# Top-k attention with an ELU feed-forward: scores three steps ahead in the opening, weight shifts a piece later in steps 8 to 10

## The chip, the cores and the metric

The kernel runs on one core of one Trainium2 chip. The metric is the device time of one execution in microseconds (us), the median of several runs. Before the change it is 1658.51 us, from three runs between 1657.33 and 1662.03.

A core has these engines: TensorE (PE) multiplies and transposes, VectorE (DVE) and ScalarE (ACT) work on rows of data, GpSimd (POOL) does small elementwise work here, and SyncE (SP) issues most transfers. Each engine works through its own list of instructions in order and waits at each for what it depends on.

## The reference

Attention over 8 batches, 8 heads, 576 positions and head size 64 keeps only the 32 largest scores of each row; its output, 4608 rows of 512, goes through a feed-forward layer with 2048 hidden columns and ELU.

```python
scores = scale * np.matmul(q, k.transpose(0, 1, 3, 2))
kth = np.partition(scores, -top_k, axis=-1)[..., -top_k:-top_k + 1]
scores = np.where(scores >= kth, scores, -1000000000.0)
attn = np.exp(scores - np.max(scores, axis=-1, keepdims=True))
attn = attn / (np.sum(attn, axis=-1, keepdims=True) + 1e-09)
x = np.matmul(attn, v)            # then (B,H,S,D) -> (B*S, H*D)
h = x @ w_in
g = np.where(h > 0.0, h, np.exp(np.minimum(h, 0.0)) - 1.0)
out = g @ w_out
```

The weights w_in and w_out come in as 64-bit floats.

## The kernel before

**Steps.** The work is a list of 144 steps (`steps`), each a tile of 128 query rows for a pair of heads. The main loop (line 667) walks over n and works at several steps at once: it computes scores for step n+2 (`scores(ahead)`), finds the 32 largest of step n (`select_row` or `select`), masks and exponentiates (`mask`), normalises step n-1 (`normalise`), transposes the weights (`turn`), and multiplies with v once a group of tiles is complete (`attend`).

**A step on each engine.** `scores(u)` is four matmul calls (L302) into two PSUM tiles, `wide[0]` and `wide[1]`, and two ACT copies (L310) into a buffer `sc`, of which there are five. The selection on DVE is four passes of the largest eight (L321, L331, or L344, L356) with three replacements between them (L325, L349), for two rows of heads. `mask` is ACT's L375, L378 and L379, or POOL's L377 in place of L375. `normalise` is POOL's L389 to L396. `turn` is nine transposes on PE (L415), in three groups (main, rest, other), each with an ACT copy (L416). The group `rest` shares the PSUM tile `wide[1]`. `attend` is L441 on PE and L468 on ACT.

**Feed-forward.** `ffn_pieces` makes a list of pieces for each block of rows: `hidden` (L513 on PE, then L523, L526, L528 on ACT) and `project` (L538 on PE, L547 on ACT, then the store). The sum that completes four hidden columns, L485 on DVE, is called a gate; it is emitted two quarter steps after its `hidden` piece. `feed` runs four times per step and takes pieces from the list by planned costs and due times. A piece is taken only if enough weights are decoded (`decoded[0]`): `project` of the first block and everything of later blocks wait for that.

**Weights.** The 64-bit weights are decoded in 32 pieces (2*NF), of which pieces 0 to 15 are w_in and 16 to 31 are w_out. Each passes through a load by SP (L153, into one of eight `raw` buffers), a clamp on POOL (`convert_first`, L174), three ACT instructions (`convert_second`, L180, L181, L183), a shift on DVE (`convert_third`, L187), and an addition on POOL (`convert_last`, L191). `hook` runs one entry of the list `decode`, `decode_piece(i)`: it issues the load of piece i+3 and the stages of pieces i, i-1, i-3 and i-4. Hooks stand between the selection passes: four per step for n = 0 to 6, none in n = 7, three per step from n = 8 until the list is empty. In this kernel entries 28 to 30 run in n = 8, 31 to 33 in n = 9, and the last, 34 and 35, in n = 10.

**Order.** For n below `tight` = 8 the framework's scheduler orders the instructions of each engine. From n = 8 on they stay in the order of the code, within a `manual_schedule`.

Of the kernel before, what the change touches and what calls it, by code (L numbers as in the profile page):

```python
# [81 lines left out]
def kernel(  # L82
# [17 lines left out]
    NHP = H // 2  # L100
    NC = dm // P
    NF = dff // P
# [48 lines left out]
    def load_weight(i):  # L151
        t = rawpool.tile([P, 2 * WN], U32, tag="raw", name="raw")
        nc.sync.dma_start(t[:], weight(i)[0])  # L153
        raw[i] = t
# [37 lines left out]

    decode = []
    decoded = [0]

    def hook():

        if not decode:
            return
        decode.pop(0)()  # L200
        if not decode:
            raws.close()
            late["f"] = ctx.enter_context(tc.tile_pool(name="f", bufs=2))
            late["g"] = ctx.enter_context(tc.tile_pool(name="g", bufs=2))
            late["x"] = ctx.enter_context(tc.tile_pool(name="xt", bufs=2))

    def decode_piece(i):
        if i + 3 < 2 * NF:
            load_weight(i + 3)
        for ago, stage in (  # L210
            (0, convert_first), (1, convert_second), (3, convert_third), (4, convert_last)
        ):
            if 0 <= i - ago < 2 * NF:
                stage(i - ago)
        decoded[0] = max(0, i - 3)

    loaded, kqT, vT = {}, {}, {}

# [18 lines left out]
    def load_v(b, hp):  # L237

        t = kvpool.tile([P, 2 * J + 2, D], FP32, tag="vT", name="vT")
        for hh in range(2):  # L240
            h = 2 * hp + hh
            nc.sync.dma_start(
                t[:, hh * J : (hh + 1) * J, :],
                v[b, h, 0:JP, :].rearrange("(p j) d -> p j d", j=J),
            )
            mine = slice(hh * R, (hh + 1) * R)
            other = slice((1 - hh) * R, (2 - hh) * R)
            nc.gpsimd.memset(t[other, 2 * J + hh, :], 0.0)
            nc.sync.dma_start(t[mine, 2 * J + hh, :], v[b, h, JP:S, :])
        vT[b, hp] = t  # L250
# [33 lines left out]
    def turn_qk(whole=False):  # L284
        while turning:
            if next(turning[0], turning) is turning:
                turning.pop(0)
            elif not whole:
                return
# [3 lines left out]
    def scores(u):  # L293

        u.sc = scpool.tile([P, 2, S], FP32, tag="sc", name="sc")
        q0 = QUERIES + u.t.qt * P
        for half in range(2):
            for h, i, rows in u.heads:
                kq = kqT[u.t.b, h // 2]
                part = slice(i * D, (i + 1) * D)  # L300
                k0 = (KEYS if i == 0 else 0) + half * HS
                nc.tensor.matmul(  # L302
                    wide[i][rows, half, 0:HS],
                    kq[part, q0 : q0 + u.t.ql],
                    kq[part, k0 : k0 + HS],
                    start=True,
                    stop=True,
                )
        for i in range(2):
            nc.scalar.activation(  # L310
                u.sc[:, i, :].rearrange("p (a s) -> p a s", a=2),
                wide[i][:, :, 0:HS], AF.Copy, scale=scale,
            )

    def select_row(u, i, decoding):
        if i == 0:
            u.first = small.tile([P, 2, 8], FP32, tag="m1", name="m1")
            u.last = small.tile([P, 2, 8], FP32, tag="m4", name="m4")
        sc = u.sc[:, i, :]
        m = u.first[:, i, :]  # L320
        nc.vector.max(m, sc)  # L321
        wk = wkpool.tile([P, S], FP32, tag=f"wk{i}", name="wk")
        cur = sc
        for r in range(TOP_K // 8 - 1):
            nc.vector.match_replace(wk[:], m, cur, TAKEN)  # L325
            cur = wk[:]
            if r < TOP_K // 8 - 2:
                m = small.tile([P, 8], FP32, tag=f"m{i}", name="m")[:]
            else:
                m = u.last[:, i, :]  # L330
            nc.vector.max(m, cur)  # L331
            if r > 0 and decoding:
                hook()
            if r != 1:
                yield
# [89 lines left out]
    def attend(g):  # L425
        t = g.tiles[0]
        ps = ps_t.tile([P, JP], FP32, tag="t", name="avps")
        n = P if t.rem else sum(x.ql for x in g.tiles)
        for k in range(2 if t.rem else 1):
            hp = 2 * g.hp + k if t.rem else g.hp  # L430
            vt = vT[t.b, hp]
            for c in range(J + 1):
                for i in range(2):
                    chunk = J if c == J else i * (J + 1) + c
                    w = g.et[:, chunk, :, :].rearrange("p a q -> p (a q)")
                    cols = slice(0, n)
                    if t.rem:
                        c0 = R * (k if i == 0 else 1 - k)
                        w = w[:, c0 : c0 + R]
                        cols = slice(k * R, (k + 1) * R)  # L440
                    nc.tensor.matmul(  # L441
                        ps[i * D : (i + 1) * D, cols],
                        vt[:, 2 * J + i if c == J else i * J + c, :],
                        w,
                        start=(c == 0),
                        stop=(c == J),
                    )
        if t.rem:
            finish(t.block, 2, slice(2 * g.hp, 2 * g.hp + 2), t.cols,
                   ps[:, 0:n].rearrange("p (a q) -> p a q", a=2))  # L450
            return
        c0 = 0
        tiles = list(g.tiles)
        while tiles:
            blk, lo, parts = tiles[0].block, tiles[0].cols.start, 0
            while tiles and tiles[0].block is blk:
                parts += 1
                hi = tiles.pop(0).cols.stop
            finish(blk, parts, g.hp, slice(lo, hi), ps[:, c0 : c0 + hi - lo])
            c0 += hi - lo  # L460
# [105 lines left out]
    blocks, tight = [], 2 * NHP  # L566
    for b in range(B):
# [28 lines left out]
        for qts in order:  # L596
# [3 lines left out]
            for qt in qts:  # L600
                n = len(steps)
# [9 lines left out]
    def at(step, fn, *args):  # L611
        todo.setdefault(step, []).append((fn, args))
# [42 lines left out]
    load_qk(0, 3)  # L655
    for hp in range(1, NHP):
        load_v(0, hp)
    decode += [lambda i=i: decode_piece(i) for i in range(2 * NF + 4)]
    at(0, start_qk, 0, 2)
    at(1, start_qk, 0, 3)  # L660

    def step(n):
        return steps[n] if 0 <= n < NS else None
# [3 lines left out]
    for n in range(NS + 3):  # L667
        for fn, args in todo.pop(n, []):
            fn(*args)
        ahead, cur, prev, done = step(n + 2), step(n), step(n - 1), step(n - 2)  # L670
        if n < tight:
            turn_qk(True)
            scores(ahead)
            for i in range(2):
                passes = select_row(cur, i, n < tight - 1)
                next(passes)
                if i == 0:
                    while closing:
                        attend(closing.pop(0))
                elif prev:  # L680
                    normalise(prev)
                    turn(prev, main)
                    turn(prev, rest)
                    turn(prev, other)
                feed(n, 0.25)
                next(passes)
                mask(cur, i, True)
                feed(n, 0.25)
            continue
        if n == tight:  # L690
            ctx.enter_context(tc.manual_schedule(engines=engines))
        passes = select(cur) if cur else iter(range(4))
        if ahead:
            scores(ahead)
        while closing:
            attend(closing.pop(0))
        next(passes)
        feed(n, 0.25)
        if prev:
            mask(prev, 0)  # L700
        turn_qk()
        next(passes)
        feed(n, 0.25)
        if done:
            turn(done, main)
            turn(done, rest)
        if prev:
            mask(prev, 1)
        next(passes)
        feed(n, 0.25)  # L710
        if done:
            turn(done, other)
        next(passes)
        if prev:
            normalise(prev)
        feed(n, 0.25)
        turn_qk(True)
# [36 lines left out]
```

## Time and profile before

| | |
|---|---|
| median of three runs | 1658.51 us |
| the profiled execution | 1660.99 us |
| its span, first to last instruction | 1659.2 us |
| PE busy | 1599.8 us (96%) |
| DVE busy | 1495.4 us (90%) |
| ACT busy | 1152.4 us (69%) |
| POOL busy | 574.9 us (35%) |
| granted PE clock, mean | 0.974 |

The profile is one execution. The span leaves out 1.8 us around the instructions. Busy shares are means over stages that differ: in the first 160 us the weights are decoded beside the attention steps; from about 1560 us on, only feed-forward work is left. The granted clock is the share of its full rate at which PE was allowed to run; a busy PE at half clock does half the work. In the rows of a timeline or a chain of waits the columns are start, length, engine, line and count. In a row of waits they are who waited for whom, the total, how often, and the longest.

### The profile page before, as it was taken

How to read it: one execution, taken by the hardware profiler on the slowest of the kernel's cores; microseconds unless marked ns; L12 is line 12 of the kernel's file. 1: busy time of each engine (PE TensorE's matmuls, PEld its weight loads, DVE VectorE, ACT ScalarE, POOL GpSimd, SP SyncE). 2: the span in 40 equal slices, each digit the busy share in tenths (PEclk: the TensorE clock that was granted, in tenths of full speed). 3: DMA queues.
4: the chain of work that ended last, by engine and by line, in shares of the span. 5: the costliest groups of instructions: out<-in, count | busy, mean ns of one | idle time of the engine just before them, and what ended most of it. 6: DMA issues, size and time to landing. Idle time of an engine off the chain costs nothing.

```text
span 1659.2 us, 25687 instructions
## 1 busy us (share of the span) xinstructions
PE 1599.8 (96%) x8528; PEld 1033.8 (62%) x8528; DVE 1495.4 (90%) x3044; ACT 1152.4 (69%) x2393; POOL 574.9 (35%) x1415
## 2 busy tenths in 40 slices
PE   5789999999999999999999999999999999999999
PEld 3566777666574757556566676756557575756564
DVE  6986999999999999999999999999999999998500
ACT  6887777678675867678667776768658585857521
POOL 4774334333333333333333233333323233332200
PEclk8588999999999999999999999999999999999999
DMA  7530110011100210011100110001200100000000
GB/s 229 184 115 7 42 39 22 7 25 40 42 1 7 50 50 8 7 28 37 36 14 1 49 36 29 0 22 36 50 13 1 34 9 29 7 7 7 7 13 13
DMA packets 101124, 56.19 MB, mean 34 GB/s; under 512 B 84096, under 2 KB 92288, under 8 KB 100992
## 3 DMA queue, kind: packets, MB, share of 16 engines
q1 hardware_dynamic: 99792, 54.26, 11.6%
q8 instruction: 68, 1.11, 0.3%
q14 instruction: 64, 0.52, 0.1%
q10 hardware_dynamic: 1200, 0.30, 0.1%
HBM read 45.09 MB, written 9.44 MB: 33 GB/s over the span
## 4 chain that ended last, share of the span: by engine, by line
PE 73%; DVE 18%; ACT 5%; POOL 2%; issue 1%; DMA 1%; SPq 0%; ACTq 0%; POOLq 0%; DVEq 0%
PE ops L538 26%; PE hps L513 23%; PE avps L441 8%; PE scps L302 7%; DVE wk L349 7%; DVE m L356 6%; PE eps L415 6%; DVE m L344 2%; PE qkps L272 1%; DVE gT L485 1%; ACT sc L379 1%; DVE wk L325 1%; PE scps L415 1%; ACT sc L378 1%; ACT et L416 1%
## 5 line engine op out<-in xcount | busy, mean ns | idle before, releaser
L356 DVE MAX8 m<-wk 128x8 f32<-128x576 f32 x816 | 574.8, 745 | 0.0
L513 PE MATMUL hps<-xT,w_in 128*128 128x256 f32 (+2 forms) x2432 | 546.9, 374 | 0.0
L538 PE MATMUL ops<-w_out,gT 128*128 128x512 f32 x1152 | 522.9, 598 | 0.0
L513 PEld LDWEIGHTS hps<-xT,w_in 128*128 128x128 f32 x2432 | 405.6, 192 | 98.2 <-issue 24.8
L349 DVE MATCH_REPLACE8 wk<-m,wk 128x576 f32<-128x576 f32 x544 | 399.3, 741 | 0.0
L538 PEld LDWEIGHTS ops<-w_out,gT 128*128 128x128 f32 x1152 | 209.0, 190 | 232.4 <-issue 219.7
L389 POOL TENSOR_SCALAR dene<-den 128x2 f32<-128x2 f32 x144 | 35.9, 249 | 815.7 <-ACT sc L379 815.2
L378 ACT ACTIVATE sc<-sc,m 128x576 f32<-128x576 f32 x288 | 226.9, 788 | 40.8 <-DVE m L356 40.5
L379 ACT ACTIVATE sc<-sc,den 128x576 f32<-128x576 f32 x288 | 223.5, 776 | 37.1 <-POOL den L377 12.5
L310 ACT ACTIVATE sc<-scps 128x576 f32<-128x576 f32 x288 | 173.3, 656 | 73.7 <-PE scps L302 73.5
L396 POOL TENSOR_SCALAR sc<-sc,rec 128x576 f32<-128x576 f32 x288 | 218.7, 770 | 14.9
L302 PE MATMUL scps<-kqT 64*128 64x288 f32 (+1 forms) x1280 | 205.9, 442 | 17.3 <-ACT kqT L278 8.7
L416 ACT COPY et<-eps 128x512 f32<-128x512 f32 x288 | 166.3, 577 | 78.5 <-PE eps L415 78.3
L441 PE MATMUL avps<-et,vT 128*64 128x256 f32 (+2 forms) x2080 | 196.8, 331 | 7.7 <-ACT et L416 7.6
L349 DVE MATCH_REPLACE8 wk<-m,sc 128x576 f32<-128x576 f32 x272 | 199.7, 741 | 0.0
L415 PEld LDWEIGHTS eps<-ident,sc 128*128 128x128 f32 x1152 | 143.6, 144 | 86.5 <-issue 47.4
L485 DVE SCALAR_TENSOR_TENSOR gT<-n,gT 128x512 f32<-128x512 f32 (+1 forms) x132 | 99.0, 750 | 108.2 <-ACT n L528 108.2
L415 PE MATMUL eps<-ident,sc 128*128 128x128 f32 x1152 | 176.8, 279 | 17.2 <-POOL sc L396 15.0
L344 DVE MAX8 m<-sc 128x8 f32<-128x576 f32 x272 | 191.0, 743 | 0.0
L441 PEld LDWEIGHTS avps<-et,vT 128*64 128x64 f32 x2080 | 124.3, 143 | 84.2 <-issue 26.1
L302 PEld LDWEIGHTS scps<-kqT 64*128 64x128 f32 (+1 forms) x1280 | 109.7, 182 | 89.4 <-issue 44.0
L523 ACT ACTIVATE n<-hps 128x512 f32<-128x512 f32 (+1 forms) x156 | 87.7, 562 | 84.2 <-PE hps L513 82.2
(49 smaller groups left out, 1086.4 us busy)
## 6 DMA issues: line engine op xcount, KB each, us to landing
kin<-in_k_dram SPq DMA_DIRECT2D x64, 128.0 KB, 2.8
raw<-in_moe_w_in_dram SPq DMA_DIRECT2D x16, 512.0 KB, 5.9
vT<-in_v_dram SPq DMA_DIRECT2D x64, 128.0 KB, 2.2
raw<-in_moe_w_out_dram SPq DMA_DIRECT2D x16, 512.0 KB, 3.5
out_dram<-osb SPq DMA_DIRECT2D x32, 256.0 KB, 2.3
qin<-in_q_dram SPq DMA_DIRECT2D x62, 128.0 KB, 2.8
kin<-in_k_dram SPq DMA_DIRECT2D x32, 32.0 KB, 2.5
vT<-in_v_dram SPq DMA_DIRECT2D x64, 16.0 KB, 2.1
```

Source lines behind the costliest of these rows:

```text
L302: nc.tensor.matmul(wide[i][rows, half, 0:HS], kq[part, q0 : q0 + u.t.ql], kq[part, k0 : k0 + HS], start=True, stop=True,)
L344: nc.vector.max(found[i], cur[i])
L349: nc.vector.match_replace(wk[i], found[i], cur[i], TAKEN)
L356: nc.vector.max(found[i], cur[i])
L378: nc.scalar.activation(sc, sc, AF.Prelu, scale=-1.0, bias=low, alpha=1.0 / STEEP)
L379: nc.scalar.activation(sc, sc, AF.Exp, scale=-STEEP, bias=gap, accum_out=u.den[:, i : i + 1])
L396: nc.gpsimd.tensor_scalar(u.sc[:, i, :], u.sc[:, i, :], rec[:, i : i + 1], 1.0, ALU.mult, ALU.mult)
L415: nc.tensor.transpose(ps[:, c * P : (c + 1) * P], sc[:, c0 : c0 + P], ident[:])
L416: nc.scalar.copy(g.et[:, chunks, u.at, :], ps[:, 0 : n * P].rearrange("p (c q) -> p c q", c=n),)
L441: nc.tensor.matmul(ps[i * D : (i + 1) * D, cols], vt[:, 2 * J + i if c == J else i * J + c, :], w, start=(c == 0), stop=(c == J),)
L513: nc.tensor.matmul(blk.h[:, f % bank, :], w_in[:, i, f * P : (f + 1) * P], blk.xT[:, i, 0:n_tok], start=(i == 0), stop=(i == NC - 1),)
L538: nc.tensor.matmul(blk.o[:], blk.gT[f // NG][:, f % NG, s * P : (s + 1) * P], w_out[:, f, :], start=(f == 0), stop=(f == NF - 1),)
```

## The change

Two things are changed.

First, the scores. In n = 0 and n = 1 scores of step n+2 are computed as before. In n = 2 they are computed for steps 4 and 5, and from n = 3 to n = 7 for step n+3. In n = 8 none are computed, since step 10 has been done; from n = 9 on it is step n+2 again.

Second, the weights. From entry `scheduled` = 28 on, that is from n = 8, the shift and the addition are done for pieces i-4 and i-5 instead of i-3 and i-4. Entry 28 does neither of the two, so no piece is skipped, and the list gets one entry more, 36, which runs in n = 10. `decoded[0]` follows.

```diff
     decoded = [0]
+    scheduled = 4 * (2 * NHP - 1)
...
-        for ago, stage in (
-            (0, convert_first), (1, convert_second), (3, convert_third), (4, convert_last)
-        ):
+        apart = 1 if i >= scheduled else 0
+        stages = [(0, convert_first), (1, convert_second)]
+        if i != scheduled:
+            stages += [(3 + apart, convert_third), (4 + apart, convert_last)]
+        for ago, stage in stages:
             if 0 <= i - ago < 2 * NF:
                 stage(i - ago)
-        decoded[0] = max(0, i - 3)
+        decoded[0] = max(0, i - 3 - apart)
...
-    decode += [lambda i=i: decode_piece(i) for i in range(2 * NF + 4)]
+    decode += [lambda i=i: decode_piece(i) for i in range(2 * NF + 5)]
...
         if n < tight:
             turn_qk(True)
-            scores(ahead)
+            if n < 3:
+                scores(ahead)
+            if n > 1:
+                scores(step(n + 3))
...
-        if ahead:
+        if ahead and n > tight:
             scores(ahead)
```

## The prediction

> Steps are numbered as in the code, n = 0 to 143; a piece is one of the 32 slices of weights; a gate is the VectorE (DVE) instruction of L485 that completes four hidden columns.
>
> **What bounds the kernel now.** I first read the busy time by stretch.
>
> ```profile
> 120.00:140.00 20.00, 16.57 (x67) 9.03 (x66) 11.06 (x23) 14.95 (x31) 11.13 (x20) 0.83 0.00 1
> 140.00:160.00 20.00, 17.41 (x95) 12.00 (x94) 15.96 (x33) 14.74 (x30) 10.58 (x21) 0.91 0.04 14
> 160.00:300.00 140.00, 139.18 (x1112) 101.47 (x1111) 138.65 (x286) 105.98 (x225) 48.53 (x132) 1.00 0.12 30
> 300.00:850.00 550.00, 538.72 (x2840) 344.65 (x2838) 550.00 (x1125) 393.17 (x818) 191.06 (x503) 0.99 0.10 26
> 850.00:1560.00 710.00, 706.51 (x3681) 448.59 (x3678) 673.95 (x1367) 499.61 (x1039) 231.53 (x609) 1.00 0.07 20
> ```
>
> Columns: length, then PE, weight loads, DVE, ACT, POOL busy, granted clock, DMA share, GB/s. From 300 to 850 us DVE never rests and PE has 11.3 us to spare; from 850 on PE is full and DVE waits. So a lead that DVE holds at 300 reaches the end if PE can make up its part from those 11.3 us. Before 160 nobody is full: there the change works. Next, what DVE waits for between 60 and 165 us:
>
> ```profile
> DVE gT L485 <- ACT n L528: 9.0, 3, 5.4
> DVE raw L187 <- POOL rec L394: 7.3, 1, 7.3
> DVE raw L187 <- ACT raw L181: 4.2, 3, 2.4
> ```
>
> The 7.3 us is one stall, 125.2 to 132.4, at the end of n = 8. The releaser named there is doubtful (POOL's L394 ended at 132.15): by the code the shift of piece 27 needs ACT's L181 of that piece, at 131.66. The 5.4 us is the first gate of the second block, at 161.35. The chain of waits tells who made both late:
>
> ```profile
> 123.89 0.67 PE eps L415 x4
> ...
> 126.14 2.29 PE scps L302 x6
> 128.42 2.33 PE avps L441 x20
> 130.75 7.69 PE ops L538 x16
> 138.45 1.22 PE scps L302 x8
> ...
> 139.71 1.19 ACT sc L310 x2
> ...
> 149.10 2.39 PE avps L441 x18
> ...
> 152.68 3.43 PE ops L538 x8
> 156.11 3.57 PE hps L513 x32
> ```
>
> DVE's 7.3 us is not on it: POOL's normalise(6) (120.60 to 124.56) releases the transposes at 123.89; then PE, then ten microseconds of ACT in order, then PE again lead to the gate. Last, PE's clock in its windows of 3.41 us:
>
> ```profile
> 121.75:125.16 3.41, 1.20 (x9) 1.00 0.00 0
> 125.16:128.58 3.42, 2.75 (x11) 0.50 0.00 0
> 145.64:149.06 3.42, 1.09 (x7) 1.00 0.00 0
> 149.06:152.47 3.41, 3.37 (x23) 0.50 0.01 2
> ```
>
> **Part 1, n = 2 to 6: one more score group early.** In n = 2 scores(4) and scores(5) stand together; after that each group takes the place of the one before it, so that the order from n = 3 to 6 is nearly as it was. Nothing waits for it to gain: DVE's only wait for scores (L321 on L310) is 0.7 us, near 35. The cost falls once, near 46 us. ACT gets two L310 copies earlier (spaced 0.53, together 1.1) and meets PE before it is done: at half clock PE's half group takes 2.29 (45.12 to 47.4, then to 49.65), so ACT waits about 1.2 and 0.95. Its mask of step 2 slips from 50.0 to about 53.3. Queued behind it are L181 of pieces 7 to 10, for which DVE's L187 waits (they stood at 49.55, 50.95, 55.45, 57.19 with 0.5 to 1.6 us of room): some 2.3 us in all. ACT waited 3.24 at 67.11 (L416 on L415) and DVE 2.40 at 70.81, both for normalise(2), which starts at 62.99 and needs L379 at about 61.7 in the new order: the delay fits. What does not fit is POOL: the changed order puts a third L174 (0.65) ahead of L191 of piece 7, which starts the chain to the next weight load (5.17 landing) and normalise(2). I take 0.55 later, between 0 (the piece lands late anyway) and 2.3. SP's queue: two k/q loads pass a weight load, 0.6 each, inside the same bounds. From 63 to 119 the order is unchanged, so +0.55 is carried.
>
> **Part 2, the shifts a piece later (n = 8 to 10).** No operation is added; hook 28 has no third and fourth stage, hook 36 is new. POOL now runs three L191 instead of four between normalise(5) and normalise(6), and the last of them needs a shift that DVE does after its second pass, without the 0.6 wait for L181 at 115.5. That puts L191 at 118.1 instead of 119.2; normalise(6) is then limited by L379 (over at 119.55) and gains 1.0. With +0.55: 0.45 early, so turn(6) starts at 123.45. On DVE, L187 of piece 27 moves behind the first pass of step 9: L344 x2 1.33, the gate, L349 x2 1.46, L356 x2 1.33 cover it, to about 131.5. ACT, without scores(10) in n = 8, has that L181 done at about 131.3, so the 7.26 shrinks to under 0.5 plus about 1.3 at the next gate (L528 ends at 128.08 whatever DVE does). Pieces 30 and 31 may wait 0.5 and 1.1. DVE alone would reach step 11 about 4.5 us earlier (150.1, against 154.57). Cover gone: had ACT not moved, the wait would be 0.2 to 1.9.
>
> **Part 3, scores(10) out of n = 8.** On PE the 2.29 at 126.14 goes: attend(6) starts at 126.1 instead of 128.4. The group went to n = 7, where it replaces scores(9). But PE is at half clock until 131.99, so more of the output matmuls runs slow (an estimated 0.86 each, twice the 0.43 of the rows at full clock): 3.4 us of them instead of 1.3, 0.9 given back. Scores(11) end at 138.1 instead of 139.55: 1.45 gained. Then ACT's in-order stretch from L310 to the last L416 of turn(7), 139.71 to 148.95 before, is unchanged in work: attend(7) at 147.6. PE stands idle 3.4 us before it, where it was 2.6.
>
> Here the clock decides. The Trainium skill (TensorE: Matmul & The Clock Gate, section HAM oscillation) says that PE falls to half rate after idle gaps above about 3.4 us. The trace is stricter: windows that were 35% and 32% busy, with gaps of 2.7 and 2.4 us, were each followed by half clock. In the changed kernel the gap before turn(6) is about 2.5 us. By the rule PE would stay at full clock, attend(6) and the output matmuls would end 2.65 us sooner, and the gain below would be 6.4; by the row it halves, and the gain is 3.75. I take the row.
>
> From attend(7), 147.6 to 149.6 (between 1.24 and 2.39 long): turn(8), now all nine transposes, to 151.2; four output columns (3.45, part at half clock) to 155.0; hidden matmuls 3.57 to 158.6; L523, L526, L528 1.8 to 160.4. The gate was ready at 161.32. In the changed order DVE has the first pass of step 11 (2.79) behind it when it waits there. Before, that pass and the gate were over at 161.94 + 2.8 = 164.75; now at 160.4 + 0.6 = 161.0. **DVE gains 3.75 us.** What is late next is PE: scores(13) start at 158.6 + 0.9 = 159.5 instead of 160.94, a lead of only 1.45 in a stretch where PE is full. The gates that follow had 2.36 (at 170.30), 2.66 and 2.45 (at 222.22) us between L528's end and L485: 1.45 + 2.36 = 3.81, just enough. PE makes up its 2.3 from the 11.3 us after 300. FFN pieces of the second block are released one quarter step later; PE's list holds the same work, so this costs only what is counted above.
>
> **Sum.** Span 1659.2 - 3.75 = 1655.45, the profiled execution 1660.99 - 3.75 = 1657.24. The median of the runs, 1658.51, lies 2.48 below that execution; from it, 1658.51 - 3.75 = **1654.8 us**.
>
> **Rivals.** (a) PE keeps full clock after 125: 6.4, 1652.1. For: 44% busy in that window now against 35%; against: a window of 56% at 691.8 was followed by half clock too. (b) The whole stall is gained or more, since ACT and PE reach the second block's gate earlier than I have it: 1658.5 - 7.3 = 1651.2, at most 7.3 + 1.6. Against: the 5.4 us wait right behind it. (c) The stall only moves: a further half-clock window at 152.5 (price 2.0) and 1 to 2.3 us of part 1 kept: 0 to 1 gained, 1658. (d) Slower: ACT runs into unfinished scores in every step from 2 to 5, not once. Price 1.2 + 0.95 = 2.15 per step, four times 8.6, plus 0.55, less 3.75: +5.4, 1663.9. It decides once ACT's L379 of the step comes later than POOL is ready for normalise (1.8 us of room at n = 2). Against it: between 60 and 100 us L310 waits for nothing, and the order there is kept. That the change does not do what it says is excluded by the changed order: DVE's L187 do stand a pass later.
>
> **Chances.** Main case 0.50 (1653 to 1657), (a) 0.20, (b) 0.14, (c) 0.08, (d) 0.08. About 0.3%, 5 us, is what a measurement of this kernel can tell from no change. Faster by more: (a), (b) and a tail of 0.04 of the main case, 0.38; within: 0.54; slower: 0.08. The range leaves out (d) and the end of (b): 1650.5 to 1659.5.
>
> **What would show it.** Right: no DVE wait above 2 us between 120 and 135; DVE's largest wait before 200 us at the second block's first gate, 5 to 7 us; PE idle over 3 us near 145; half clock near 125 to 132; an ACT wait of over 1 us for L302 near 47. Wrong: normalise(2) later than 64.5, or a gate between 165 and 230 that waits over 1 us.

## The result and the profile after

The changed kernel takes 1656.28 us, median of 12 runs (1652.84 to 1658.83), against 1660.45 us of the kernel before, median of 12 runs beside them (1657.33 to 1663.60). The ratio is 0.9975, 95% interval 0.9965 to 0.9985: 4.2 us faster, between 2.5 and 5.8. Measured again on another occasion (below) it was 0.9956, 0.9944 to 0.9969, which is 7.3 us. The forecast gain was 3.75 us.

The profiled execution took 1652.84 us, with a span of 1651.1 us: 8.1 us less than the span before. It was the fastest of its 12 runs, so one pair of profiles shows about twice what the medians do. A good part of this study is about why.

Busy time by stretch, columns as before (length, PE, weight loads, DVE, ACT, POOL, granted clock, DMA share, GB/s), after the change:

```profile
120.00:140.00 20.00, 18.14 (x93) 11.34 (x93) 17.47 (x34) 18.03 (x38) 11.52 (x20) 0.97 0.00 1
140.00:160.00 20.00, 17.63 (x123) 13.01 (x122) 15.82 (x34) 14.54 (x31) 10.61 (x21) 0.91 0.04 15
160.00:300.00 140.00, 139.45 (x1109) 101.97 (x1107) 140.00 (x288) 106.81 (x228) 49.00 (x135) 1.00 0.13 32
```

From 120 to 140 DVE is busy 17.47 us instead of 11.06, and the granted clock is 0.97 instead of 0.83. From 160 to 300 DVE never rests now (140.00 of 140.00; 138.65 before, where the wait at the second block's first gate lasted until 161.35). What DVE waits for between 60 and 165 us:

```profile
DVE gT L488 <- ACT n L531: 10.4, 3, 4.3
DVE raw L187 <- ACT raw L181: 2.6, 2, 1.7
```

The line numbers have moved by three: L488 is the gate, L531 the last ACT instruction in front of it. The 7.3 us stall at L187 is gone. The chain of waits over the same stretch:

```profile
123.98 0.45 PE eps L418 x4
...
126.50 1.30 PE avps L444 x18
127.81 7.06 PE ops L541 x16
134.87 1.22 PE scps L305 x8
136.09 0.04 issue
136.13 1.19 ACT sc L313 x2
...
145.54 2.40 PE avps L444 x18
...
149.40 3.44 PE ops L541 x8
152.84 3.58 PE hps L516 x32
...
158.08 0.69 DVE gT L488
```

It is the chain of before, without the 2.29 us of scores ahead of attend(6): PE, then ACT in order from 136.13 to 145.5, then PE, then the gate. The output matmuls are 0.63 us shorter (7.06 against 7.69): before, their first 1.2 us ran at half clock, here none did. One gate of the first block and then the gates of the second, from the timeline of DVE:

```profile
122.53 1.09 DVE L488 SCALAR_TENSOR_TENSOR gT<-n,gT 128x512 f32<-128x512 f32 x1 [4.34 <-ACT n L531]
...
158.08 0.69 DVE L488 SCALAR_TENSOR_TENSOR gT<-n,gT 128x512 f32<-128x512 f32 x1 [4.18 <-ACT n L531]
164.26 0.69 DVE L488 SCALAR_TENSOR_TENSOR gT<-n,gT 128x512 f32<-128x512 f32 x1
171.75 0.67 DVE L488 SCALAR_TENSOR_TENSOR gT<-n,gT 128x512 f32<-128x512 f32 x1
```

The bracket is the wait and its releaser. The gate of the first block waits 4.34 us, where it waited 2.60 before (at 121.68). The second block's first gate still waits 4.18 us; the next two wait for nothing, but L531 ended only 0.03 and 0.36 us before them. Step 12 on DVE, before and after:

```profile
170.89 1.41 DVE L344 MAX8 m<-sc 128x8 f32<-128x576 f32 x2
```

```profile
164.87 1.41 DVE L347 MAX8 m<-sc 128x8 f32<-128x576 f32 x2
```

DVE's lead over the execution before (start of a step then, minus now) is 6.55 us at step 9, 4.85 at step 11, 6.02 at step 12, 6.07 at step 79, 7.71 at step 80, 7.77 at step 140, and the end is 8.1 earlier.

### The profile page after: what moved, and what is told of

It reads as the page before. It is cut to its first block, busy times and chain, and to the rows that moved or that the text cites. A ratio compares the mean times of both kernels' runs of the same rounds, so it can differ in the third digit from the quotient of the medians.

```text
span 1651.1 us, 25682 instructions
## 1 busy us (share of the span) xinstructions
PE 1592.8 (96%) x8528; PEld 1031.8 (62%) x8528; DVE 1496.6 (91%) x3044; ACT 1152.7 (70%) x2393; POOL 576.4 (35%) x1415
## 4 chain that ended last, share of the span: by engine, by line
PE 67%; DVE 24%; ACT 4%; POOL 2%; issue 1%; DMA 1%; SPq 0%; ACTq 0%; POOLq 0%; DVEq 0%
PE ops L541 24%; PE hps L516 22%; DVE wk L352 9%; DVE m L359 8%; PE avps L444 8%; PE scps L305 7%; PE eps L418 5%; DVE m L347 3%; DVE gT L488 1%; DVE wk L328 1%; PE qkps L275 1%; DVE m L334 1%; ACT sc L382 1%; PE scps L418 1%; ACT sc L381 1%
## 5 line engine op out<-in xcount | busy, mean ns | idle before, releaser
L392 POOL TENSOR_SCALAR dene<-den 128x2 f32<-128x2 f32 x144 | 34.6, 240 | 818.9 <-ACT sc L382 818.5
L313 ACT ACTIVATE sc<-scps 128x576 f32<-128x576 f32 x288 | 173.3, 657 | 73.6 <-PE scps L305 73.4
L399 POOL TENSOR_SCALAR sc<-sc,rec 128x576 f32<-128x576 f32 x288 | 219.4, 772 | 15.0 <-POOL rec L397 0.2
L305 PE MATMUL scps<-kqT 64*128 64x288 f32 (+1 forms) x1280 | 204.1, 443 | 18.3 <-ACT kqT L281 9.1
L488 DVE SCALAR_TENSOR_TENSOR gT<-n,gT 128x512 f32<-128x512 f32 (+1 forms) x132 | 99.3, 752 | 107.6 <-ACT n L531 107.6
L418 PEld LDWEIGHTS eps<-ident,sc 128*128 128x128 f32 x1152 | 144.3, 144 | 82.0 <-issue 49.6
L418 PE MATMUL eps<-ident,sc 128*128 128x128 f32 x1152 | 176.5, 279 | 13.0 <-POOL sc L399 11.7
L305 PEld LDWEIGHTS scps<-kqT 64*128 64x128 f32 (+1 forms) x1280 | 109.4, 183 | 89.0 <-issue 44.3
```

Source lines behind the costliest of these rows:

```text
L305: nc.tensor.matmul(wide[i][rows, half, 0:HS], kq[part, q0 : q0 + u.t.ql], kq[part, k0 : k0 + HS], start=True, stop=True,)
L313: nc.scalar.activation(u.sc[:, i, :].rearrange("p (a s) -> p a s", a=2), wide[i][:, :, 0:HS], AF.Copy, scale=scale,)
L399: nc.gpsimd.tensor_scalar(u.sc[:, i, :], u.sc[:, i, :], rec[:, i : i + 1], 1.0, ALU.mult, ALU.mult)
L418: nc.tensor.transpose(ps[:, c * P : (c + 1) * P], sc[:, c0 : c0 + P], ident[:])
```

## The experiments

Theory T: the lead is decided at the second block's first gate. It comes from two things, the chain PE, ACT, PE in front of that gate, and the place of the gate in DVE's order, one selection pass later than before; the 7.3 us stall by itself is worth little, and PE's half-clock windows shift each execution by up to 2 us. Rival R: the removed stall is the gain.

| | ratio to before, 95% interval | span of its profile |
|---|---|---|
| changed kernel | 0.9975 (0.9965 to 0.9985) | 1651.1 |
| a_again | 0.9956 (0.9944 to 0.9969) | 1653.0 |
| e1_shift_only | 0.9973 (0.9962 to 0.9983) | 1653.7 |
| e2_scores_only | 0.9996 (0.9987 to 1.0005) | 1658.3 |
| e3_double_at_7 | 0.9962 (0.9949 to 0.9976) | 1652.6 |
| e4_turn_other_early | 0.9953 (0.9940 to 0.9965) | 1654.8 |
| e6_before_gate_later | 0.9986 (0.9977 to 0.9995) | 1660.9 |
| e7_after_gate_earlier | 0.9972 (0.9960 to 0.9983) | 1655.4 |
| e8_after_gates_later | 0.9942 (0.9928 to 0.9956) | 1648.9 |
| e9_gates_and_turn | 0.9947 (0.9934 to 0.9959) | 1648.2 |
| e10_after_fill | 0.9986 (0.9978 to 0.9995) | 1655.7 |
| e11_e8_fill | 0.9973 (0.9964 to 0.9982) | 1653.9 |

0.001 is 1.7 us. Spans of single profiles differ by some us for reasons that no edit made: e6, whose order is that of the kernel before up to step 11, reached normalise(6) at 124.08 us against 120.60. So I compare the stretch from the start of normalise(6) (POOL, L389 or L392), in two legs: to the first gate of the second block, and from there to the start of step 12. The third column is PE's half clock between 124 and 156 us.

| | normalise(6) at | half clock | to the gate | gate to step 12 | sum |
|---|---|---|---|---|---|
| before | 120.60 | 10.2 | 40.75 | 9.54 | 50.29 |
| changed | 120.39 | 3.4 | 37.69 | 6.79 | 44.48 |
| a_again | 121.39 | 6.8 | 38.71 | 6.79 | 45.50 |
| e1 | 121.27 | 0 | 38.51 | 6.79 | 45.30 |
| e2 | 122.41 | 10.2 | 39.44 | 9.53 | 48.97 |
| e3 | 122.15 | 6.8 | 38.15 | 6.79 | 44.94 |
| e4 | 122.58 | 10.2 | 39.40 | 6.80 | 46.20 |
| e6 | 124.08 | 12.6 | 41.63 | 6.17 | 47.80 |
| e7 | 120.17 | 10.2 | 40.27 | 9.58 | 49.85 |
| e8 | 120.32 | 6.8 | 38.85 | 3.39 | 42.24 |
| e9 | 120.39 | 3.4 | 38.19 | 3.39 | 41.58 |
| e10 | 119.69 | 3.4 | 43.33 | 6.79 | 50.12 |
| e11 | 121.06 | 6.8 | 43.22 | 3.39 | 46.61 |

**The changed kernel once more.**

> The changed kernel once more, for a second profile. Theory T (the second block's first gate is set by the chain from turn(6) through ScalarE to turn(8); DVE's 7.3 us stall by itself is worth little; the half-clock windows of PE move the result by up to 2 us): about 4 us under the kernel before (ratio 0.9965 to 0.9985), the gate at 157.5 to 161.5 according to where the half-clock windows fall. If the gain is real but its size in the first pair of profiles (8.1 us) was chance, the span of this profile is 1652 to 1657. Theory R (the 7.3 us stall is the gain): the same total, and the lead of DVE at step 12 is 6 to 7.3 us, whatever the windows.

The gain was larger, 7.3 us, the lead smaller: 4.00 us at step 12. The profile (PE and DVE) reads:

```profile
129.21 7.63 PE L541 MATMUL ops<-w_out,gT 128*128 128x512 f32 x16
136.77 1.24 PE L305 MATMUL scps<-kqT 64*128 64x288 f32 x8
...
147.46 2.40 PE L444 MATMUL avps<-et,vT 128*64 128x128 f32 x18 [2.32 <-ACT et L419]
```

```profile
160.10 0.69 DVE L488 SCALAR_TENSOR_TENSOR gT<-n,gT 128x512 f32<-128x512 f32 x1 [6.02 <-ACT n L531]
```

Scores(11) end at 138.0, attend(7) goes on at 147.46, the gate runs at 160.10. The same program had them at 136.0, 145.54 and 158.08 in the other execution; here PE went to half clock at 126.9 for 3.4 us, there it did not. R, which expected a lead of 6 to 7.3 whatever the clock does, is wrong in that.

**One part alone.** Only the shift a piece later (all diffs are against the changed kernel, except that of e6):

```diff
-            if n < 3:
-                scores(ahead)
-            if n > 1:
-                scores(step(n + 3))
+            scores(ahead)
...
-        if ahead and n > tight:
+        if ahead:
```

> Only the shift a piece later; scores two steps ahead everywhere as before. T: the 7.3 us stall is gone here too, but scores(10) still lie on PE before attend(6), so DVE waits longer at the second block's first gate, and the gain is about 2.5 to 3.3 us (ratio about 0.998). R: the whole gain or more, 4 to 7.3 us (ratio 0.9955 to 0.9975).

Only the scores three ahead (the rest as in the changed kernel, `scheduled` never reached):

```diff
-    scheduled = 4 * (2 * NHP - 1)
+    scheduled = 10 ** 6
...
-    decode += [lambda i=i: decode_piece(i) for i in range(2 * NF + 5)]
+    decode += [lambda i=i: decode_piece(i) for i in range(2 * NF + 4)]
```

> Only the scores three steps ahead; shifts as before. T: 0.5 to 1.5 us faster (ratio about 0.9995), the stall at L187 of piece 27 stays, between 4 and 8 us. R: no gain, or slower by the 0.4 to 1.4 us that the early steps cost.

DVE's waits from 60 to 170 us in e1, then in e2:

```profile
DVE gT L488 <- ACT n L531: 10.1, 4, 4.2
DVE raw L187 <- ACT raw L181: 3.9, 2, 2.4
DVE raw L187 <- POOL rec L397: 0.7, 1, 0.7
```

```profile
DVE gT L488 <- ACT n L531: 11.1, 3, 5.8
DVE raw L187 <- POOL dene L395: 6.1, 1, 6.1
DVE raw L187 <- ACT raw L181: 3.4, 3, 1.4
```

The shift takes the stall away, the scores do not. In time the shift alone gave 4.5 us (2.8 to 6.3), more than the 2.5 to 3.3 that T had named and not to be told from the whole change; the scores alone gave 0.7 (2.2 faster to 0.8 slower), as T had it. By these two runs alone R looks better than T. The table of legs says what the shift brought: the second leg is 6.79 instead of 9.54, because the shift also changes the count of decoded weights, on which the pieces of the second block wait, and so moves the gate one pass of DVE down. That has to be taken apart from the stall.

**The gate's place, apart from the stall.** The kernel before with the first two gates of the second block a pass later, and the changed kernel with the first a pass earlier. `close_gates(k)` emits the gates that are at least k quarter steps old; without these edits k is 6 in n = 7 to 9 and 2 elsewhere, before the change as after it.

```diff
-        close_gates(2 if n < tight - 1 or n > tight + 1 else 6)
+        close_gates({tight - 1: 6, tight: 6, tight + 1: 6, tight + 3: 3}.get(n, 2))
```

> The kernel before, with the first two gates of the second block emitted one selection pass later, nothing else. T: DVE does one pass (2.8 us) in front of the gate instead of standing there, so the gate's wait falls from 5.4 to about 2.6, step 12 starts 2.7 us earlier than before, and the time falls by about as much (ratio about 0.9984), although the 7.3 us stall at L187 stays. R (the removed stall is the gain): no gain, within 0.5 us of before (ratio 1.000).

```diff
-        close_gates(2 if n < tight - 1 or n > tight + 1 else 6)
+        close_gates({tight - 1: 6, tight: 6, tight + 1: 6, tight + 3: 1}.get(n, 2))
```

> As changed, but the second block's first gate a selection pass earlier, where the kernel before has it. T: the stall stays gone, yet DVE waits 7 to 8.8 us at that gate instead of 4.2 to 6.0, and the lead at step 12 is 2.7 us smaller (1.3 to 3.3); the time is 2.7 us above the changed kernel (ratio to before 0.9975 to 0.999). R: as the changed kernel (ratio 0.9956 to 0.9975).

The waits of DVE from 60 to 165 us, e6 first, then e7:

```profile
DVE raw L187 <- POOL rec L394: 7.7, 1, 7.7
DVE gT L485 <- ACT n L528: 5.8, 2, 3.2
DVE raw L187 <- ACT raw L181: 4.5, 3, 2.4
```

```profile
DVE gT L488 <- ACT n L531: 15.7, 3, 9.4
DVE raw L187 <- ACT raw L181: 3.0, 3, 1.2
```

In e6 both gates of that list are of the first block. The second block's first gate comes behind the window:

```profile
165.71 0.69 DVE L485 SCALAR_TENSOR_TENSOR gT<-n,gT 128x512 f32<-128x512 f32 x1 [2.99 <-ACT n L528]
```

e6 keeps the whole stall (7.7), and its gate waits 2.99 us instead of 5.39. From normalise(6) to step 12 it needs 47.80 us, against 50.29 before, although it had more half clock. (Its second leg is shorter than 6.79 because its second gate stands behind the start of step 12.) In time it is 2.3 us faster than before (0.8 to 3.8); R had expected nothing, T 2.7.

e7 has no stall. But its first gate of the second block waits 9.4 us, 4.0 more than before, and a gate of the first block 4.40 instead of 2.60: most of the time that the stall took is now waited at these two. From normalise(6) to step 12 e7 needs 49.85 us, against 50.29 before. So in this pair of profiles, with 10.2 us of half clock in both, the removed stall and the scores taken out of n = 8 are together worth 0.4 us in that stretch. That is against R.

The time of e7 is not. In the median it gained 4.7 us (2.8 to 6.6), more than T allowed (1.7 to 4.2), within what R had named, and not to be told from the 4.2 and 7.3 of the changed kernel. By the time alone, this run does not show that the gate's place matters in the changed kernel. Of its profile's 3.8 us over before (span 1655.4 against 1659.2), 0.9 were there at step 12 and 1.5 at step 60; 2.0 came between the starts of steps 79 and 80, and 0.4 at the end. That later part is taken up below.

**The step with two groups of scores.** Moved from n = 2 to n = 7:

```diff
-            if n < 3:
-                scores(ahead)
-            if n > 1:
+            scores(ahead)
+            if n == tight - 1:
                 scores(step(n + 3))
```

> As changed, but the step with two groups of scores is n = 7 instead of n = 2, so the early steps are as before. T: normalise(2) to normalise(5) start as before, at 63.0 to 107.9 (the changed kernel was 0.4 to 1.4 later); normalise(6) about as in the changed kernel; gate and time within 1 us of it (ratio to before 0.9965 to 0.998). R: the same, since the stall is gone here as well. If the early cost had been carried to the gate, it is 0.9 to 1.4 us faster than the changed kernel.

The time is that of the changed kernel (0.9962, between its 0.9975 and 0.9956). Normalise(2) starts at 63.33, in the changed kernel at 63.36, and in e1 and e6, whose opening is that of the kernel before, at 63.70 and 64.11. Normalise(4) stands at 93.59 here, 93.36 in the changed kernel, 91.94 before and 94.88 in e6. So my expectation of 63.0 to 107.9 failed, and the 0.4 to 1.4 us by which the changed kernel is later there cannot be called a cost of the early scores: the kernel before differs by 3 us from itself.

**ScalarE's stretch in front of attend(7).** In n = 9 the third transposed group of turn(7) right behind the second:

```diff
             turn(done, main)
             turn(done, rest)
+        if done and n == tight + 1:
+            turn(done, other)
         if prev:
             mask(prev, 1)
```

> As changed, but in n = 9 the third group of turn(7) stands right behind the second, ahead of the mask of the second row. T (the gate is set by the chain through ScalarE's stretch in front of attend(7)): attend(7) starts up to 2.3 us earlier, the second block's first gate 1 to 1.4 us earlier at equal clock, the time about 1 us under the changed kernel (ratio to before 0.995 to 0.997). Rival: the mask that is pushed back makes normalise(8), and with it turn(8), later by as much; then the gate and the time stay where they are in the changed kernel (gate 158 to 160).

PE's 2.3 us wait in front of attend(7) is gone; turn(8) waits 2.50 us for POOL's L399 of normalise(8) in its place, as the rival said. At equal half clock (10.2) the first leg is 39.40 against e7's 40.27, 0.9 shorter (T: 1 to 1.4). In the median the time is 0.9953, next to the changed kernel's 0.9956 from the second occasion: the 1 us that T had named can't be told.

**Gates held back further.** The changed kernel with four quarter steps instead of two in n = 10 to 24:

```diff
-        close_gates(2 if n < tight - 1 or n > tight + 1 else 6)
+        close_gates(2 if n < tight - 1 or n > 3 * tight else 6 if n < tight + 2 else 4)
```

> As changed, but in n = 10 to 24 each gate is held back by four quarter steps instead of two. T: the wait at the second block's first gate falls by a pass, from 4.2 to 6.0 us down to 1.4 to 3.2, step 12 starts another 2.8 us earlier, the gates behind it wait little, and the time is 1.5 to 2.8 us under the changed kernel (ratio to before 0.994 to 0.9965). Rival: PE, which is full from 160 to 300 us, is then the bound; the lead is given back at scores or gates before step 40, and the time is that of the changed kernel.

```profile
159.17 0.69 DVE L488 SCALAR_TENSOR_TENSOR gT<-n,gT 128x512 f32<-128x512 f32 x1 [3.43 <-ACT n L531]
166.66 0.67 DVE L488 SCALAR_TENSOR_TENSOR gT<-n,gT 128x512 f32<-128x512 f32 x1
```

The gate waits 3.43 us (T: 1.4 to 3.2). The second leg is 3.39: the gate stands yet another pass and a sum later. The lead is 8.33 us at step 12 and still 7.85 at step 79, where the rival had it given back before step 40. No gate and no score waits between 165 us and step 79; there, at 850.56, a gate waits 1.7 us, as one does in step 79 of every profile here (3.7 before). At 0.9942 e8 has the lowest ratio of this study, 9.6 us under the kernel before (7.3 to 12), but its interval overlaps that of a_again. With e4's early third group of turn(7) added (e9):

> e8_after_gates_later and e4_turn_other_early together: gates of n = 10 to 24 held back by four quarter steps, and the third group of turn(7) right behind the second. T: from normalise(6) to the start of step 12 it takes 41 to 42.5 us (before 50.3, e8 42.2), since the chain to the first gate is about 0.9 shorter at equal clock and the gate still waits; time 0.5 to 1 us under e8 (ratio to before 0.9925 to 0.995). Rival: PE is already the bound after e8, then the time is that of e8 (0.9942) within 0.5 us.

It is 0.9947: the same as e8. The legs are 38.19 and 3.39, their sum 0.7 shorter than in e8, but with one half-clock window less. The lead over e8 is 0.6 us at step 12 and 0.7 at step 140, and the gate in step 79 waits as long as in e8 (1.73 us in both). So the profiles do not show PE giving anything back, as the rival has it; the times cannot tell 0.7 us.

**Filling PE's gaps.** Five matmuls, which the trace shows as ten instructions, at each of two places on PE, in the changed kernel (e10) and in e8 (e11):

```diff
+        if n == tight + 2:
+            for _ in range(5):
+                nc.tensor.matmul(
+                    wide[1][:, 0, HS:JP], ident[:], w_in[:, 0, 0 : JP - HS],
+                    start=True, stop=True,
+                )
         while closing:
             attend(closing.pop(0))
...
+        if n == tight:
+            for _ in range(5):
...
         if done:
             turn(done, main)
```

> As changed, plus five matmuls (128 rows, 224 columns, into an unused part of a PSUM tile) ahead of turn(6) in n = 8 and five ahead of attend(7) in n = 10, where PE has its gaps of about 2.2 and 2.3 us; they add work that the reference does not need. Theory C (the gaps bring the half clock of 124 to 132 and 145 to 149 us): about 1 us of each gap is filled at no cost, there is no half-clock window between 124 and 156 us, normalise(6) to the first gate of the second block takes 36.5 to 37.3 us (37.7, 38.7 in the two profiles of the changed kernel), and the time is 1 us under the changed kernel. Rival: the clock does not answer to these gaps, the windows stay, and the matmuls cost up to 1 us.

> e8_after_gates_later with the same ten matmuls added. Theory C: no half-clock window between 124 and 156 us, the first gate 1 to 2 us nearer to normalise(6) than in e8 (38.85), time 0.5 to 1.5 us under e8 (ratio to before 0.993 to 0.9945). Rival: windows as in e8, time as e8 or up to 1 us more.

The edit did something else than I meant. PE in e10, the lines around attend(7):

```profile
148.19 3.27 PE L703 MATMUL scps<-w_in,ident 128*128 128x224 f32 x10 [3.77 <-ACT sc L313]
151.38 1.83 PE L444 MATMUL avps<-et,vT 128*64 128x128 f32 x20
```

The added matmuls write unused columns of a PSUM tile of which ACT's L313 still reads the others, and L313 stands at the end of ACT's stretch; so they wait 3.77 us, and then delay attend(7) by 3.2. In n = 8 they fell between the output matmuls (130.99 to 132.88), not into the gap. So theory C was not tested. But they test T: both first legs grow, to 43.33 and 43.22, 4.4 to 5.6 us over e8, a_again and the changed kernel, DVE still has its lead at step 11 in e10 (5.46 us, with no stall), waits 9.74 at the gate, and is left with 1.08 at step 12. The time goes up to 0.9986 and 0.9973: of the changed kernel's 4.2 or 7.3 us, 2.3 are left (0.8 to 3.7), and of e8's 9.6, 4.5 (3.0 to 6.0). A longer chain in front of the gate takes about half of the gain away, with the stall gone. This, with e6, is the evidence that the removed stall is not the gain by itself.

## Why the prediction was right, and where not

The sign held. The size held in the first series, 3.75 us forecast and 4.2 measured (2.5 to 5.8); in the second it was 7.3 (5.2 to 9.3), above the forecast. The mechanism, a gate set by the chain PE, ACT, PE and standing one pass later, held up to step 12. What came behind step 12 was not in the sum, so the closeness of 3.75 to 4.2 is in part luck. The main case is best compared with a_again, since there PE went to half clock near 127, as in the forecast, though for 3.4 us only.

- **Stall and gate.** L187 of piece 27 ran at 131.38 without a wait (7.26 before). The second block's first gate waited 4.18 and 6.02 us (5 to 7 forecast). But a gate of the first block waited 4.34 and 4.08 until 122.53 and 123.54, instead of 2.60: the sign "no wait above 2 us between 120 and 135" failed there, and in the first profile this wait, not the second block's, was the largest from 60 us on (in the opening L187 waited up to 10 us, before the change too). DVE reached that gate 0.9 us earlier than before, and its input came 0.85 us later.
- **The gate a pass later.** Costed at one pass, 2.79; measured 2.75 in the profiles (9.54 less 6.79), and alone, in e6, 2.3 us of time. This is the largest single term, and the sum had it only as a clause of part 2.
- **ACT's stretch unchanged, and the chain behind it.** From the end of scores(11) to attend(7): 9.5 forecast, 9.5 in the changed kernel and in a_again. From attend(7) to the gate's input n being ready: 12.8 forecast, 12.5 and 12.6 measured. Right.
- **Scores(11) at 138.1.** In a_again they end at 138.0, attend(7) follows at 147.46 (147.6), n is ready at 160.07 (160.4), and the lead at step 12 is 4.00 (3.75). Two errors cancel in this: attend(6) began 0.8 us late (126.88 instead of 126.1), and the output matmuls took 7.63 us where the sum has 7.69 + 0.9, since the half clock ended at 130.2 and not at 131.99. The 0.45 us by which turn(6) was to start earlier never enters the sum of part 3; turn(6) began at 123.82 and 124.14, not at 123.45.
- **Gates behind it "just enough".** Slack 0.03 and 0.36 us; no wait at any gate until step 79. Right.
- **Part 1's +0.55 in the opening.** Not to be told from the difference between two executions. ACT's wait for L305 near 47 us is there, 1.08 us; whether it costs stays open.
- **PE idle over 3 us near 145.** It was 2.37 and 2.32; PE now waits 0.84 us earlier, for ACT's L313 inside turn(7) (L418 at 137.47), which the forecast did not have. Wrong.
- **Half clock from 125 to 132.** In the first profile PE kept full clock from 121.3 to 145.2, as in rival (a). There scores(11) ended at 136.0 instead of 138.1, and the lead was 6.02 instead of 3.75 (rival (a) had 6.4). The gap of 2.5 us ahead of turn(6), from which the forecast took its half clock, was not there: PE had been at half clock from 111.0 to 121.3 and was still busy with hidden matmuls when turn(6) began. In a_again the gap was 1.32. The step "I take the row" failed in treating gap and row as properties of the kernel: they differ between executions.
- **Nothing changes after 165 us.** The sum put this at nothing, and in these profiles that is wrong by about 2 us: from step 12 to the end the lead grows from 6.02 to 8.1 us, in a_again from 4.00 to 6.2, most of it between the starts of steps 79 and 80 (6.07 to 7.71). In windows of 3.41 us, in step 63, the kernel before:

```profile
691.77:695.18 3.41, 1.90 (x11) 0.93 (x12) 3.41 (x8) 3.32 (x9) 0.41 (x2) 1.00 0.00 0
695.18:698.59 3.41, 3.41 (x17) 1.94 (x18) 3.41 (x9) 0.98 (x2) 2.59 (x6) 0.50 0.02 5
```

and the changed one at the same place of the program:

```profile
684.42:687.83 3.41, 2.34 (x16) 1.52 (x14) 3.41 (x8) 3.11 (x7) 0.38 (x2) 1.00 0.00 0
687.83:691.25 3.42, 3.12 (x22) 1.52 (x20) 3.42 (x8) 2.28 (x5) 2.18 (x6) 1.00 0.02 5
```

Both have a wait of 1.1 to 1.2 us ahead of scores there, and one of 0.3 behind. In the kernel before both waits fell into one window, and the next was at half clock, so that the 18 matmuls of an attend took 4.06 us instead of 2.37. The delay appears at the gate at 860.42, where DVE waited 3.7 us before and 2.1 after. From step 69 to 81 the lead over that execution grows by 1.6 to 2.0 us in the ten profiles that do not have this window, and by 0.4 in e1 and e6, which have it. So some 1.3 us of each comparison with this one profile is that window, by this difference. Whether the kernel before has it in most of its executions, in which case it would be part of the measured gain, is open: the three profiles with scores two ahead in the opening (before, e1, e6) all have it, the ten others don't.

What stays open besides: how the gain splits between the two parts. The shift alone gave 4.5 us with an interval from 2.8 to 6.3; its one profile had no half clock at all from 124 to 156 us, which flatters its first leg (38.51). The scores alone shortened that leg by 1.3 us with as much half clock (39.44 against 40.75), and the time by 0.7, which is not clear of zero. And e7's 4.7 us: its one profile has 0.9 us by step 12 and 3.0 behind it, and how much of the later part comes from the change is open.

## What to carry to other kernels

When a stall disappears, ask what the same engine waits for next. Here, in e7, the stall of 7.3 us was gone, and two gates waited 5.8 us more; in e6 a selection pass moved ahead of the gate paid, although the stall stayed. A wait that another chain sets is shortened by putting other work in front of it, or by shortening that chain; an earlier stall of the engine that waits can then be worth little: 0.4 us by step 12 in the one pair of profiles that tells. And a single pair of profiles is a poor measure of a change of 4 us: align them at an event in front of the stretch in question, and set the clock of each beside it.

## What the runs showed of the hardware

PE's granted clock changes at the edges of a grid of 3.41 us (in these profiles half clock lasts 3.41, 6.83, 10.24 us and so on), and that grid stands differently against the start in each execution (edges at 145.2 and 148.6 in the changed kernel, 147.3 and 150.7 in a_again). The gap in front of attend(7) is 2.31 to 2.38 us in the nine profiles whose edits leave it there; in eight of them half clock follows, in e1 it does not. The changed kernel, then e1:

```profile
141.75:145.17 3.42, 1.43 (x10) 0.70 (x10) 3.42 (x9) 3.30 (x7) 1.60 (x5) 1.00 0.00 0
145.17:148.58 3.41, 3.04 (x22) 2.71 (x23) 3.41 (x8) 2.02 (x5) 3.32 (x6) 0.50 0.01 2
```

```profile
143.53:146.94 3.41, 2.07 (x15) 1.18 (x13) 3.41 (x8) 3.29 (x8) 1.14 (x3) 1.00 0.00 0
146.94:150.35 3.41, 2.43 (x28) 2.26 (x29) 3.41 (x9) 3.02 (x7) 3.16 (x6) 1.00 0.01 2
150.35:153.77 3.42, 3.21 (x8) 1.01 (x7) 3.42 (x8) 3.33 (x8) 3.23 (x5) 1.00 0.00 0
```

In the changed kernel the gap lies in one window; PE is busy 1.43 us of it (42%), and the next window is at half clock. In e1 the grid cuts the gap in two; PE is busy 2.07 and 2.43 us (61% and 71%), and nothing follows. For this gap, then, the place of the grid goes with what follows. PE's busy share in one window does not tell it in general. In e3 ahead of turn(6) (PE alone), then in e1 in step 63:

```profile
121.08:124.49 3.41, 2.59 (x10) 1.00 0.00 0
124.49:127.91 3.42, 3.02 (x14) 0.50 0.00 0
```

```profile
686.26:689.67 3.41, 2.35 (x12) 1.24 (x11) 3.41 (x8) 3.23 (x7) 0.19 (x1) 1.00 0.00 0
689.67:693.09 3.42, 3.42 (x16) 1.53 (x16) 3.42 (x8) 1.79 (x5) 2.66 (x7) 0.50 0.02 5
```

Windows that were busy for 2.59 and 2.35 us were followed by half clock, and the changed kernel's window with 2.34 us (684.42, above) was not. What decides is open.

Half clock goes with a longer first leg: 37.69 us with 3.4 us of it, 38.15 to 38.85 with 6.8 (e3, a_again, e8), 40.27 with 10.2 (e7), some 0.5 to 2 us for each window. The rule that the prediction weighed (the Trainium skill, TensorE: Matmul & The Clock Gate, section HAM oscillation: idle gaps above about 3.4 us) would have kept full clock after a gap of 2.3 us; half clock in eight of nine profiles decides against it. That the gaps bring the half clock is read from these rows; the experiment that was to fill them did not do so.
